# Test products of 12-bit operands and splitting operations behind the last product of a Fourier mixing and SwiGLU kernel

## The chip, the cores and the metric

One core of one Trainium2 chip. The metric is the device time of one execution in microseconds (us), the median of the runs shown.

## What is computed

The reference filters each sequence in the frequency domain and then applies a SwiGLU block to every token.

```python
batch, seq, dim = (8, 3008, 256)          # filter: 1505 frequencies x 256
X = np.fft.rfft(x, axis=1)
Y = X * (filt_r + 1j * filt_i)[None]
y = np.fft.irfft(Y, n=3008, axis=1).astype(np.float32)
x = y.reshape(24064, 256)                 # d_ff = 1536
g = x @ w_gate
silu = g * (1.0 / (1.0 + np.exp(-g)))
out = (silu * (x @ w_val) @ w_out).astype(np.float32)
```

## The kernel before, in words

The transform is factored: 3008 = 47 x 64, small table products in several stages, the spectrum multiplied with the filter in between, and the way back by the same kind of stages. The eight sequences are worked one after the other; while the SwiGLU block of one runs, the transform of the next is put in between in small pieces.

The SwiGLU block of a sequence is 12 steps: 4 chunks of tokens times 3 groups of hidden blocks. A `Group` object is one such step. Its products (`product`, line 1125) multiply combined weights in `wt_t` with the tokens `y` (P, Q) or with sums of them in `y_t` (A, B, E); 188 columns a product. ScalarE and VectorE turn the sums in PSUM into the hidden tile `h` (lines 1140 to 1172), VectorE and GpSimd combine `h` for the output (`S`, lines 312 and 315), and `project` (line 1223, 376 columns a product) multiplies with `wo_t` and adds into the output tile `o` on VectorE (line 312). Finished output tiles are transposed by VectorE (line 1194) and stored (line 1208).

The order of all this is written out by hand in the string `SCHEDULE`, one token an operation, and `pin` (`tc.keep_in_program_order`) holds every operation to that order on its engine. The work behind the last step stands in `LAST`: the rest of `S` and `W` (products), `o` (additions), `z1.o` and `z2.o` (transposes), `x0.o` to `X5.o` (stores, dealt in turn to the queues of SP, ScalarE and GpSimd, line 1208). The last operations of `LAST` are the end of the kernel. Nothing follows them.

Memory: `pool` opens a pool of tiles that lives to the end. `wo_t`, `wt_t`, `y_t` (128 x 18 x 188) and `lent` (128 x 7168) are whole-kernel tiles. The pools `hp` (four `h` buffers of 128 x 7 x 376), `np` (small tiles) and `op` (two output tiles) are opened late, when the start's own pool has closed. PSUM tiles come from `bank(name)`, eight banks in turn. `idle` (line 578) issues products that nobody reads; the kernel has 20 of them, all in its first 90 us. An unread ScalarE operation stands at line 1289.

All products have f32 operands. In the trace a product of f32 operands is two records, and so is its weight load.

Of the kernel before, what the change touches and what calls it, by code (L numbers as in the profile page):

```python
# [41 lines left out]
FP32 = mybir.dt.float32  # L42
U32 = mybir.dt.uint32
AF = mybir.ActivationFunctionType
ALU = mybir.AluOpType
# [155 lines left out]
def kernel(  # L201
# [10 lines left out]
    nc = tc.nc  # L212
# [10 lines left out]
    def pool(name, bufs, space=None):  # L223
        kw = {} if space is None else {"space": space}
        return ctx.enter_context(tc.tile_pool(name=name, bufs=bufs, **kw))
# [13 lines left out]
    y_t = cpool.tile([128, 3 * len(PAIRS), TQ], FP32)  # L239

    lent = cpool.tile([128, 14 * NV * C], FP32)
# [51 lines left out]
    pin = tc.keep_in_program_order  # L293
# [963 lines left out]
    with tc.tile_pool(name="start", bufs=1) as spool0:  # L1257
# [12 lines left out]
        n = 0  # L1270
        while n < NPR - 1:
            pair = ORDER[n][0] in "ABE" and ORDER[n + 1][0] in "ABE"
# [92 lines left out]
    def reload_sums(k, d):  # L1365
        pin(nc.sync.dma_start(out=sums_of(y_t, d), in_=sums_of(yt_dram[k], d)))

    hpool = pool("hp", 4)
    npool = pool("np", 1)
    opool = pool("op", 1)  # L1370

# [69 lines left out]
    for b in range(B):  # L1443
# [41 lines left out]
        for step in range(NCHUNK * NG + (b == B - 1)):  # L1485
# [16 lines left out]
            for place, token in enumerate(SCHEDULE):  # L1502
# [3 lines left out]
                op = token.rstrip("'")  # L1506
# [13 lines left out]
                elif op[0] == "t":  # L1520
                    n = int(op[1])
                    ps = pieces_before if old else pieces
# [21 lines left out]
                if b == 1 and step < 4 and op in FILTER_AT:  # L1544
                    n = FILTER_AT.index(op)
# [11 lines left out]
    for op in LAST:  # L1557
        if op[0] == "S":
            older.step(op, nc.gpsimd if op[1] == "2" else nc.vector)
        else:  # L1560
            older.project(op, True)
# [1 line left out]
_INS = ['x', 'filt_r', 'filt_i', 'moe_w_gate', 'moe_w_val', 'moe_w_out']  # L1563
_OUTS = [((B * S, C), 'float32')]
# [25 lines left out]
```

## Time and profile before

| | |
|---|---|
| two runs | 2789.07 and 2793.10 us |
| median | 2791.09 us |
| span of the profiled execution | 2788.6 us |
| the profiled execution's own time | not given beside its span |
| mean granted TensorE clock | 0.997 |
| end of TensorE's last product | 2779.6 us |
| end of VectorE's last operation | 2782.5 us |
| end of GpSimd's last store issue | 2786.0 us |

How to read the profile: times are microseconds from the start of the span, and ns where a mean is given. PE is TensorE's products, PEld its weight loads, DVE VectorE, ACT ScalarE, POOL GpSimd, and a name with q the engine's instruction queue. A line of groups has line, engine, operation, output and inputs with their shape, count, then busy us and mean ns of one, then the idle time ahead of them with what ended it. A line of the timeline has start, length and count; several equal instructions in a row are one line. A line of stretches has from and to, length, busy time and count of PE, PEld, DVE, ACT and POOL, the granted clock, the share of the DMA engines and GB/s.

### The profile page before, as it was taken

What the parts mean: (1) busy time and instruction counts of PE and PEld (TensorE: products, weight loads), DVE (VectorE), ACT (ScalarE), POOL (GpSimd) and SP (SyncE); (2) the same over time, 40 slices, a digit from 0 to 9 for tenths busy, and PEclk for the clock granted to TensorE, in tenths of its full rate; (3) what the DMA queues carried; (4) which work ended last, traced back from release to release, by engine and by line L of the source; (5) the groups of instructions that cost most, each with busy time, mean ns of one, the idle gap of its engine ahead of it and who ended that gap; (6) DMA issues with size and microseconds to landing.
All of it is one profiled execution on the core that took longest, in us unless ns stands there. A gap on an engine that the chain in (4) does not pass through costs nothing.

```text
span 2788.6 us, 51410 instructions
## 1 busy us (share of the span) xinstructions
PE 2748.3 (99%) x16952; PEld 2249.3 (81%) x16952; DVE 2081.7 (75%) x4703; ACT 1514.6 (54%) x4086; POOL 1647.4 (59%) x1801
## 2 busy tenths in 40 slices
PE   8999999999999999999999999999999999999998
PEld 6777887888878888788878888878887888888886
DVE  7888777777687777777778777777777777676666
ACT  5776454555555555555555555555554555555553
POOL 4786576566545665556654566555655566555554
PEclk9999999999999999999999999999999999999999
DMA  8688877878676776777767777668767677655543
GB/s 216 218 273 267 282 240 243 265 243 263 205 211 208 253 244 190 212 238 229 247 184 233 220 249 223 207 194 264 243 213 201 215 239 237 183 156 147 156 137 83
DMA packets 383488, 608.47 MB, mean 218 GB/s; under 512 B 197118, under 2 KB 266652, under 8 KB 383048
## 3 DMA queue, kind: packets, MB, share of 16 engines
q1 hardware_dynamic: 364410, 574.18, 65.9%
q10 hardware_dynamic: 16174, 25.50, 3.6%
q0 software_dynamic: 2640, 5.51, 0.7%
q8 instruction: 137, 2.24, 0.3%
q14 instruction: 127, 1.04, 0.1%
HBM read 484.45 MB, written 118.12 MB: 216 GB/s over the span
## 4 chain that ended last, share of the span: by engine, by line
PE 89%; DVE 3%; POOL 2%; ACT 1%; DMA 1%; issue 1%; SPq 0%; POOLq 0%; DVEq 0%; ACTq 0%
PE wa L1125 25%; PE wk L1125 17%; PE wA L1223 16%; PE we L1125 12%; PE wG L1223 8%; PE wF L1223 4%; PE wpd L1043 2%; PE wqc L807 1%; PE wqb L819 1%; PE wqa L727 1%; POOL h L315 0%; POOL out_dram L1208 0%; PE wpa L889 0%; DVE we L315 0%; DVE y L319 0%
## 5 line engine op out<-in xcount | busy, mean ns | idle before, releaser
L1125 PE MATMUL wa<-y_t,wt_t 128*128 128x188 f32 x4464 | 883.5, 324 | 10.5 <-DVE wa L1147 5.5
L1125 PEld LDWEIGHTS wa<-y_t,wt_t 128*128 128x128 f32 x4464 | 746.0, 190 | 102.9 <-issue 14.7
L1125 PEld LDWEIGHTS wk<-y,wt_t 128*128 128x128 f32 x2976 | 494.4, 190 | 125.2 <-issue 36.7
L1125 PE MATMUL wk<-y,wt_t 128*128 128x188 f32 x2976 | 575.6, 326 | 1.4 <-ACT f L1140 1.4
L315 POOL TENSOR_TENSOR h<-h 128x376 f32<-128x376 f32 x572 | 560.1, 1000 | 15.1 <-DVE h L312 14.9
L1223 PE MATMUL wA<-h,wo_t 128*128 128x376 f32 x1532 | 549.0, 481 | 3.4 <-POOL h L315 1.8
L1125 PE MATMUL we<-y_t,wt_t 128*128 128x188 f32 x2232 | 432.4, 323 | 2.4 <-DVE we L319 1.6
L315 POOL TENSOR_TENSOR D<-f,f 128x376 f32<-128x376 f32 x288 | 280.5, 985 | 252.0 <-ACT f L1140 245.4
L312 POOL TENSOR_TENSOR h<-h 128x376 f32<-128x376 f32 x190 | 183.2, 984 | 408.0 <-DVE h L1172 402.2
L315 DVE TENSOR_TENSOR we<-we,m 128x376 f32<-128x376 f32 x576 | 317.3, 552 | 91.6 <-PE we L1125 51.4
L1125 PEld LDWEIGHTS we<-y_t,wt_t 128*128 128x128 f32 x2232 | 369.1, 190 | 4.9 <-DVE we L319 2.8
L1223 PEld LDWEIGHTS wA<-h,wo_t 128*128 128x128 f32 x1532 | 278.0, 190 | 106.6 <-POOL h L315 5.4
L1160 ACT COPY m<-wa 128x376 f32<-128x376 f32 x576 | 275.4, 478 | 110.8 <-PE wa L1125 105.0
L1167 ACT ACTIVATE u<-we 128x188 f32<-128x188 f32 x576 | 188.9, 328 | 188.5 <-DVE we L315 179.1
L1223 PE MATMUL wG<-h,wo_t 128*128 128x376 f32 x768 | 273.9, 479 | 0.0
L319 DVE SCALAR_TENSOR_TENSOR y<-wk,c 128x376 f32<-128x376 f32 x480 | 246.7, 540 | 33.7 <-ACT c L1144 29.5
L1167 ACT ACTIVATE g<-wa 128x188 f32<-128x188 f32 x576 | 187.4, 326 | 143.8 <-PE wa L1125 141.6
L1144 ACT COPY c<-wk 128x376 f32<-128x376 f32 x288 | 136.9, 475 | 234.5 <-PE wk L1125 228.1
L1156 ACT COPY we<-y 128x376 f32<-128x376 f32 x480 | 218.9, 480 | 42.9 <-DVE y L1049 24.7
L1140 ACT ACTIVATE f<-wk 128x376 f32<-128x376 f32 x288 | 145.1, 504 | 168.6 <-PE wk L1125 108.3
L1172 DVE TENSOR_TENSOR h<-we,u 128x188 f32<-128x188 f32 x576 | 198.7, 345 | 35.1 <-ACT u L1167 21.9
L1172 DVE TENSOR_TENSOR h<-wa,g 128x188 f32<-128x188 f32 x576 | 196.1, 344 | 26.2 <-ACT g L1167 26.1
(194 smaller groups left out, 3532.0 us busy)
## 6 DMA issues: line engine op xcount, KB each, us to landing
wt_t<-w_all SPq DMA_DIRECT2D x174, 896.0 KB
wt_t<-w_all SPq DMA_DIRECT2D x174, 768.0 KB
lent<-filter SPq DMA_DIRECT2D x36, 1024.0 KB
quads<-lent SPq DMA_DIRECT2D x96, 256.0 KB
d<-lent ACTq DMA_DIRECT2D x84, 256.0 KB
t<-d SPq DMA_DIRECT2D x112, 192.0 KB
lent<-quads SPq DMA_DIRECT2D x144, 128.0 KB
lent<-raw SPq DMA_DIRECT2D x144, 128.0 KB
```

The source lines that it names most:

```text
L312: return eng.tensor_tensor(out=dst, in0=a, in1=b, op=ALU.add)
L315: return eng.tensor_tensor(out=dst, in0=a, in1=b, op=ALU.subtract)
L319: return nc.vector.scalar_tensor_tensor(out=dst, in0=a, scalar=-1.0, in1=b, op0=ALU.mult, op1=ALU.subtract)
L1043: pin(nc.tensor.matmul(out=outs_[h][32 * j:32 * j + 32, i], lhsT=back_t[0][r, ts(m, 32)], rhs=t[r, j], start=i == 0, stop=True, skip_group ...
L1125: pin(nc.tensor.matmul(out=ps[:, z], lhsT=self.wt[:, SLOT[p], z], rhs=rhs, start=start and z == 0, stop=True, skip_group_check=True))
L1140: pin(act.mul(self.small(f"f{i}", f"f{i}", 1), t[f"k{i}"], -1.0))
L1144: pin(act.copy(out=self.small(f"c{i}", f"c{i}", 1), in_=t[f"k{i}"]))
L1156: pin(act.copy(out=self.bank(f"e{at}"), in_=t[f"y{at}"]))
L1160: pin(act.copy(out=self.small(f"m{at}", "m", 4), in_=t[f"a{at}"]))
L1167: pin(act.activation(out=self.small(op, "g", 3, 1)[:, 0], in_=ps[:, 1], func=AF.Silu))
L1172: pin(v.tensor_tensor(out=dst, in0=ps[:, 0], in1=g, op=ALU.mult))
L1223: pin(nc.tensor.matmul(out=self.tiles[at], lhsT=wo_t[:, JB * q + i, WO[p], :], rhs=self.hs[i][:, HID[p]], start=start and i == 0, stop=Tru ...
```

## The change

The three late pools get an `ExitStack` of their own, which is closed behind `LAST`. In the room that they leave a pool `test` is opened with two tiles of the type F32R, a four-byte type whose values hold 12 significant bits. VectorE fills both (0 times `lent`, plus 0.75). TensorE runs 18 products each of 376, 188, 256 and 512 columns into one bank each, then 16 of 376 columns in turn into two banks. Then come three rounds of 14 operations on ScalarE, VectorE and GpSimd, which copy, multiply, apply Silu and split values into a 12-bit part and the rest; they write into `y_t` and the second test tile. Nothing of it is read for the output; output, products and stores ahead of it stay as they are.

```diff
-    hpool = pool("hp", 4)
-    npool = pool("np", 1)
-    opool = pool("op", 1)
+    late = ExitStack()
+
+    def late_pool(name, bufs):
+        return late.enter_context(tc.tile_pool(name=name, bufs=bufs))
+
+    hpool = late_pool("hp", 4)
+    npool = late_pool("np", 1)
+    opool = late_pool("op", 1)
...
             older.project(op, True)
+
+    late.close()
+    F32R = mybir.dt.float32r
+    tpool = pool("test", 1)
+    wr = tpool.tile([128, 768], F32R, name="test_w")
+    xr = tpool.tile([128, 1024], F32R, name="test_x")
+    pin(nc.vector.tensor_scalar(out=wr, in0=lent[:, 0:768], scalar1=0.0, scalar2=0.75, op0=ALU.mult, op1=ALU.add))
+    pin(nc.vector.tensor_scalar(out=xr, in0=lent[:, 0:1024], scalar1=0.0, scalar2=0.75, op0=ALU.mult, op1=ALU.add))
+    for n in (376, 188, 256, 512):
+        ps = bank(f"test_{n}")
+        for i in range(18):
+            pin(nc.tensor.matmul(out=ps[:, 0:n], lhsT=wr[:, ts(i % 6, 128)],
+                                 rhs=xr[:, 32 * i % 512:32 * i % 512 + n],
+                                 start=i == 0, stop=True, skip_group_check=True))
+    pair = [bank(f"test_pair_{i}") for i in range(2)]
+    for i in range(8):
+        for j in range(2):
+            pin(nc.tensor.matmul(out=pair[j][:, 0:376], lhsT=wr[:, ts(i % 6, 128)],
+                                 rhs=xr[:, 32 * i + 300 * j:32 * i + 300 * j + 376],
+                                 start=i == 0, stop=True, skip_group_check=True))
+    zt = y_t.rearrange("p s n -> p (s n)")
+    lam = 4096.0
+
+    def at(i, n=376):
+        return zt[:, 376 * i:376 * i + n]
+
+    stt = dict(scalar=-lam, op0=ALU.mult, op1=ALU.add)
+    hi, lo = xr[:, 0:376], xr[:, 376:752]
+    for r in range(3):
+        pin(nc.scalar.activation(out=at(0), in_=pair[0][:, 0:376], func=AF.Copy, scale=1.0 / lam))
+        pin(nc.vector.scalar_tensor_tensor(out=at(1), in0=pair[1][:, 0:376], scalar=1.0 + 1.0 / lam,
+                                           in1=at(0), op0=ALU.mult, op1=ALU.subtract))
+        pin(nc.scalar.activation(out=at(2), in_=at(1), func=AF.Silu))
+        pin(nc.vector.tensor_tensor(out=at(3), in0=at(1), in1=at(2), op=ALU.mult))
+        pin(nc.scalar.activation(out=hi, in_=at(3), func=AF.Copy, scale=1.0 - 2.0 ** -13))
+        pin(nc.gpsimd.tensor_tensor(out=lo, in0=at(3), in1=hi.bitcast(FP32), op=ALU.subtract))
+        pin(nc.vector.scalar_tensor_tensor(out=xr[:, 376:752], in0=lo.bitcast(FP32), in1=hi.bitcast(FP32), **stt))
+        pin(nc.gpsimd.tensor_tensor(out=at(5), in0=at(1), in1=at(2), op=ALU.mult))
+        pin(nc.vector.tensor_tensor(out=lo, in0=at(3), in1=hi.bitcast(FP32), op=ALU.subtract))
+        pin(nc.gpsimd.tensor_tensor(out=at(4, 752), in0=at(0, 752), in1=at(2, 752), op=ALU.subtract))
+        pin(nc.vector.tensor_tensor(out=at(6, 752), in0=at(0, 752), in1=at(2, 752), op=ALU.subtract))
+        pin(nc.scalar.activation(out=xr[:, 0:752], in_=at(4, 752), func=AF.Copy, scale=1.0 - 2.0 ** -13))
+        pin(nc.vector.tensor_scalar(out=hi, in0=at(3), scalar1=1.0 - 2.0 ** -13, scalar2=None, op0=ALU.mult))
+        pin(nc.gpsimd.tensor_scalar(out=hi, in0=at(3), scalar1=1.0 - 2.0 ** -13, scalar2=None, op0=ALU.mult))
```

## The prediction

> **What bounds the kernel now.** I read the page first, its busy shares and the chain that ended last.
>
> ```profile
> PE 2748.3 (99%) x16952; PEld 2249.3 (81%) x16952; DVE 2081.7 (75%) x4703; ACT 1514.6 (54%) x4086; POOL 1647.4 (59%) x1801
> ...
> PE 89%; DVE 3%; POOL 2%; ACT 1%; DMA 1%; issue 1%; SPq 0%; POOLq 0%; DVEq 0%; ACTq 0%
> ```
>
> TensorE is busy for 99% of the span and carries 89% of the chain. Cover from TensorE ends, though, where its last product ends, and everything that is added stands behind that point. So the timeline of the end comes second.
>
> ```profile
> 2770.85 1.43 PE L1223 MATMUL wF<-h,wo_t 128*128 128x376 f32 x4
> 2772.11 1.43 PE L1223 MATMUL wG<-h,wo_t 128*128 128x376 f32 x4
> ...
> 2778.18 1.43 PE L1223 MATMUL wG<-h,wo_t 128*128 128x376 f32 x4
> ...
> 2780.61 3.82 SPq L1208 DMA_DIRECT2D out_dram<-o  x8
> 2780.61 4.23 ACTq L1208 DMA_DIRECT2D out_dram<-o  x8
> ...
> 2781.50 1.04 DVE L1194 STREAM_TRANSPOSE o<-o 128x384 f32<-128x384 f32 x2
> 2783.00 3.05 POOL L1208 DMA_DIRECT2D out_dram<-o  x5 [0.28 <-issue]
> ```
>
> The reader is to see four ends: TensorE at 2779.6 us, VectorE at 2782.54, ScalarE's queue at 2784.84, GpSimd's last store issue at 2786.05. The span ends at 2788.6; the stores of this line take 1.9 to 2.5 us to land, which fills most of the last 2.55 us. All that can still cover added work is these 9 us.
>
> Third, the stretches, for the granted clock (the column after the five engines; the first three lines are the end, the last two the start of the kernel):
>
> ```profile
> 2782.00:2784.00 2.00, 0.00 (x0) 0.00 (x0) 0.54 (x2) 0.00 (x0) 1.72 (x4) 0.96 1.00 168
> 2784.00:2786.00 2.00, 0.00 (x0) 0.00 (x0) 0.00 (x0) 0.00 (x0) 2.00 (x4) 0.50 0.93 150
> 2786.00:2788.60 2.60, 0.00 (x0) 0.00 (x0) 0.00 (x0) 0.00 (x0) 0.06 (x1) 0.50 0.12 25
> ...
> 4.00:8.00 4.00, 4.00 (x22) 2.76 (x20) 0.00 (x0) 0.82 (x1) 0.00 (x0) 1.00 0.98 244
> ...
> 12.00:16.00 4.00, 4.00 (x22) 4.00 (x21) 2.02 (x7) 1.76 (x3) 1.10 (x3) 0.53 1.05 241
> ```
>
> By 2784 us the clock has fallen to 0.50. New products that begin there begin at half speed, as those at 12 us did.
>
> Fourth, the groups with shapes kept apart, for the durations:
>
> ```profile
> L1160 ACT COPY m<-wa 128x376 f32<-128x376 f32 x576 | 275.4, 478 | 110.8 <-PE wa L1125 105.0
> L1076 ACT ACTIVATE y_t<-y 128x376 f32<-128x376 f32 x64 | 29.4, 509 | 7.0 <-PE we L1125 7.0
> L319 DVE SCALAR_TENSOR_TENSOR y<-wk,c 128x376 f32<-128x376 f32 x480 | 246.7, 540 | 33.7 <-ACT c L1144 29.5 <-ACT we L1156 3.7 <-issue 0.2
> L315 POOL TENSOR_TENSOR h<-h 128x376 f32<-128x376 f32 x572 | 560.1, 1000 | 15.1 <-DVE h L312 14.9
> L312 POOL TENSOR_TENSOR y_t<-y 128x564 f32<-128x564 f32 x31 | 43.1, 1389 | 0.0
> ...
> L312 DVE TENSOR_TENSOR h<-h 128x376 f32<-128x376 f32 x2 | 1.0, 544 | 0.0
> ...
> L315 POOL TENSOR_TENSOR h<-h 128x376 f32<-128x376 f32 x2 | 2.4, 1216 | 14.9 <-DVE h L312 14.9
> ```
>
> **The change, part by part.** It removes nothing and moves no instruction. Giving the three late pools a stack of their own changes when they close and issues nothing; I cost it at zero. All else comes behind the last transpose on VectorE, the last product on TensorE, the last store issue on ScalarE's and GpSimd's queues. SP gets nothing.
>
> Step 1, two VectorE fills (768 and 1024 columns), which the products wait for. The TENSOR_SCALAR rows are 128x256: 283 ns the quickest, 611 in a large group. VectorE's additions grow by 1.01 ns a column (550 ns at 376, 740 at 564). At half of that slope the two take 0.54 + 0.67 = 1.2 us, at all of it 0.80 + 1.06 = 1.9, and from 611 ns 2.5. I take 1.5. They start at 2782.54, so the products start at 2784.1. The stores are still being issued meanwhile; nobody waits for these fills but TensorE.
>
> Step 2, 88 products: 18 each of 376, 188, 256 and 512 columns, 18 x 1332 = 23,976, and 16 of 376, 6,016; in all 29,992 columns. Before, each f32 product shows as two records: 20 idle products in the code stand as 40 records in the trace. Four records of 376 columns follow at 1.26 us, 0.84 ns a column and record. With two records each, as f32, the test takes 50.3 us; with one each at the same pace 25.2. From below, each product needs its weights: the shortest weight load of the trace (24x32, 103 ns) times 88 is 9.1 us. No row shows a product with such operands. The operands are narrower than f32's, so I put two records in a rival and take the middle of 9.1 and 25.2, 17.2 us. To that comes the clock: 32 equal records (L902) took 3.71 us at clock 1.00 and 6.38 at 0.53, 2.7 more; six records of 512 columns at the very start took 2.0 more than their warm pace; a half clock from 12 to 21.6 us would cost 4.8. I take 2.7. Products: 19.9 us, ending at 2804.0.
>
> Here a rule bears on the unknown. The Trainium skill, page "FP8 and Floating Point Precision", section "TensorE Precision Notes", says true FP32 takes four passes through the array and that there is a reduced form that truncates to a narrower float. The two records fit with four passes of two each. A single pass would be a quarter of 50.3, an estimate of 12.6 us, and the total 4.6 us lower. No run here shows that these operands take the reduced form.
>
> Step 3, three rounds of 14 operations. Nothing covers them: each round starts with ScalarE reading the pair that TensorE writes last, and the next round starts with ScalarE, behind its 752-column copy of the round before. The path through a round: ScalarE copy out of PSUM 0.48; VectorE 0.54; ScalarE Silu over 376, by the 376-column ACTIVATE, 0.51; VectorE product 0.54; ScalarE scaling 0.49; GpSimd difference 1.00. Together 3.56. Then GpSimd has its next two in its own order while VectorE runs three: a 376-column product and a 752-column difference. Alone the second takes 1.39 + 188 x 2.1 ns = 1.79; the row with VectorE beside it has 1.22 for 376, so 1.22 and 1.79 x 1.22 = 2.18. Then ScalarE's copy over 752: 509 ns and 376 x 0.78 (362 ns at 188) = 0.80. The sum is 7.76. Handoffs between engines in the chain of the end are 0.02 to 0.04 us, to GpSimd 0.15 to 0.28; seven in a round are 0.33. A round is 8.1 us, three 24.3. The last two, VectorE's scaling (0.45) and GpSimd's over the same tile (0.57, between its COPY rows of 390 ns for one column and 630 for 512), end the last round only, since otherwise they run beside ScalarE's and VectorE's next steps: 1.1 with handoffs. Step 3 is 25.4 us. Ends: GpSimd undisturbed (1.00 and 1.79) with short handoffs, 7.3 a round, 22.9 in all; VectorE and GpSimd taking strict turns, 3.56 + 0.54 + 1.00 + 0.54 + 1.79 + 0.94 + 0.80 + 0.33 = 9.5 a round, 29.6.
>
> On this the skill's page "SBUF — State Buffer", section "SBUF: two separate sides", has a rule that speaks against my sum: VectorE with two SBUF inputs and GpSimd take turns on one pair of ports, and the loser waits out the whole instruction. That would be the 29.6. The row is milder for GpSimd: 1.22 for 1.00 in the tail, while VectorE's two took 2.57 for 1.09. I stay with the row.
>
> Step 4, the end. The stores have long landed when the last operation ends, so of the 2.55 us only what is left over 1.9 to 2.5 of landing remains: 0.05 to 0.65. I take 0.5; the high end is 2.55.
>
> **The sum.** 2784.1 + 19.9 + 25.4 + 0.5 = 2829.9 against 2788.6: 41.3 us more span. The profiled execution shows its span, not its own total; the median of the two runs is 2.5 us over the span. I take that to stay: 2791.1 + 41.3 = 2832.4 us, 1.5% more.
>
> **Rivals.** First, two records for each test product, as before: 33.1 us more, 2865.5, 2.7% slower than before. For it: every product in this trace has two, whatever its shape. Against: the operands hold fewer bits. It decides once the products take over 31.7 us (17.2 and the 14.5 left to 2%), 0.36 us each on average; f32 would have 0.57. Chance 0.09.
>
> Second, a late start. The test tiles lie in memory of closed pools. They need 7 KB a partition and the first pool's first buffer has 10.5, read last by products long ended; that speaks for 2784.1. If instead the fills wait for the output tiles' stores, they start at 2786.05 + 2.3 = 2788.35, 5.75 later: 2838.1. Chance 0.14.
>
> Third, strict turns of VectorE and GpSimd: 4.2 more, 2836.6. Chance 0.10.
>
> Fourth, unread operations are left out and nothing changes: 2791. Against it: the unread idle products (40 records) and an unread ScalarE operation on a 128x1 tile at the start do stand in the trace. Chance 0.02.
>
> **How the numbers follow.** The forecast, 2832.4, has 0.63. Its own range is 2820.4 (2783.8 + 9.1 + 2.0 + 22.9 + 0.1, 29.3 more span) to 2840.4 (products at 25.2). Two high ends together, which reach 2846 and above, have 0.02. The range for 8 in 10 takes in the late start and the strict turns with part of their sums with 25.2: 2820 to 2847. 2%, 55.8 us or 2846.9, is about what a measurement of this kernel can tell from no change. Slower: 0.09 + 0.02, and 0.01 for prices that no row bounds, 0.12; faster: 0.01, since nothing is removed; same: 0.87.
>
> **What would show it.** One record for each test product, granted clock 0.5 at their start, about 20 us between the first and the last; ScalarE, VectorE and GpSimd idle for that time except the fills and the stores; then three equal rounds of about 8 us in which GpSimd has the most time, and an end within 1 us of GpSimd's last operation. Products up to 2779.6 us must stand as they do. Two records, a gap before the fills, or GpSimd operations well over 1.2 and 2.2 us would each prove a step wrong.

## The result, and the profile after

The changed kernel takes 2830.55 us (2829.24 and 2831.87) against 2791.09, 1.4% more by the medians; the ratio on record is 1.0149, 95% interval 1.0113 to 1.0184. That is clear of noise, though under the 2% that the prediction took as the line between slower and the same. The forecast was 2832.4. The profiled execution took 2829.24 us with a span of 2827.4; every run here stands 1.8 us over its span, not 2.5.

First the busy shares and the chain, from the page of the changed kernel:

```profile
PE 2764.3 (98%) x17040; PEld 2264.2 (80%) x17040; DVE 2098.9 (74%) x4723; ACT 1521.9 (54%) x4098; POOL 1662.4 (59%) x1813
...
PE 87%; DVE 3%; POOL 2%; ACT 2%; DMA 1%; issue 1%; SPq 0%; POOLq 0%; ACTq 0%; DVEq 0%
```

TensorE has 88 records more, 16952 and 17040: one for each of the 88 test products, so unread operations are not left out (the fourth rival). The chain that ended last, in order of time, then shows that nothing of the addition is hidden but the fills and the first products, which lie beside the stores:

```profile
2781.03 0.57 DVE test_w L1573
2781.60 0.60 DVE test_x L1574
...
2782.34 14.41 PE wtest L1578 x72
2796.75 2.58 PE wtest_pair L1584 x15
...
2799.36 0.49 ACT y_t L1596
...
2802.25 0.98 POOL test_x L1602
...
2803.25 1.32 DVE test_x L1603
...
2804.59 2.01 DVE test_x L1605
...
2806.71 0.83 ACT test_x L1608
2807.54 0.43 ACT y_t L1596
```

The last line is the second round's first operation. The chain counts it from the end of the operation ahead of it; in the timeline it starts at 2807.48, 8.12 us behind the first round's, and the third follows 8.20 later. The stretches give the clock, as in the prediction:

```profile
2782.00:2784.00 2.00, 1.66 (x5) 1.69 (x6) 0.20 (x1) 0.00 (x0) 2.00 (x4) 0.50 0.93 163
...
2786.00:2788.00 2.00, 2.00 (x8) 2.00 (x7) 0.00 (x0) 0.00 (x0) 0.00 (x0) 0.50 0.00 0
2788.00:2790.00 2.00, 2.00 (x18) 2.00 (x17) 0.00 (x0) 0.00 (x0) 0.00 (x0) 0.87 0.00 0
2790.00:2792.00 2.00, 2.00 (x20) 2.00 (x19) 0.00 (x0) 0.00 (x0) 0.00 (x0) 1.00 0.00 0
```

The granted clock falls to 0.50 at 2781.7 us, 3.6 us behind the last product of the old work, and steps to 1.00 at 2788.5 (hence the mean of 0.87 from 2788 to 2790). All 18 products of 376 columns, the last of which starts at 2787.8, ran at half clock, 0.313 us apart. At full clock the same width is 0.17 us apart (the 16 of the pair).

Last comes the timeline of VectorE and GpSimd in the second round, where the path parts from the one forecast:

```profile
2810.45 0.98 POOL L1602 TENSOR_TENSOR test_x<-y_t,test_x 128x376 fp32r<-128x376 f32 x1 [1.26 <-ACT test_x L1601]
2811.38 0.97 POOL L1604 TENSOR_TENSOR y_t<-y_t 128x376 f32<-128x376 f32 x1
2811.46 1.31 DVE L1603 SCALAR_TENSOR_TENSOR test_x<-test_x 128x376 fp32r<-128x376 f32 x1 [1.64 <-POOL test_x L1602]
2812.44 1.95 POOL L1606 TENSOR_TENSOR y_t<-y_t 128x752 f32<-128x752 f32 x1
2812.80 2.00 DVE L1605 TENSOR_TENSOR test_x<-y_t,test_x 128x376 fp32r<-128x376 f32 x1
2814.72 0.93 DVE L1607 TENSOR_TENSOR y_t<-y_t 128x752 f32<-128x752 f32 x1
```

GpSimd is hardly slowed (0.97 and 1.95 us), but VectorE's 376-column operations take 1.31 and 2.00 instead of 0.55. Each of them ends 0.4 us behind the GpSimd instruction that was running: 2811.38 + 0.97 = 2812.35 against 2812.77, and 2812.44 + 1.95 = 2814.39 against 2814.80. ScalarE's copy waits for VectorE (L1605), not for GpSimd.

Put against the forecast, each counted from the end of TensorE's last product (2779.6 us before, 2778.1 here):

| term | forecast us | measured us |
|---|---|---|
| to the first test product | 4.5 | 4.25 |
| 88 products | 19.9 | 17.0 |
| three rounds and the two last operations | 25.4 | 26.2 |
| end | 0.5 | 1.9 |
| sum | 50.3 | 49.3 |

The terms are 1.0 us under the forecast. Another 1.5 us is where the last product fell, and 0.7 the time over the span (1.8 for 2.5); together the profiled execution is 3.2 us under 2832.4. In the profiled executions of these runs it ended between 2776.8 and 2782.6 us, and once at 2789.6, with the same work ahead of it, so totals of single runs differ by that much.

### The profile page after: what moved, and what is told of

Its sections match the earlier page's. It is cut to its first block, busy times and chain, and to the rows that moved or that the text cites. A ratio compares the mean times of both kernels' runs of the same rounds, so it can differ in the third digit from the quotient of the medians.

```text
span 2827.4 us, 51641 instructions
## 1 busy us (share of the span) xinstructions
PE 2764.3 (98%) x17040; PEld 2264.2 (80%) x17040; DVE 2098.9 (74%) x4723; ACT 1521.9 (54%) x4098; POOL 1662.4 (59%) x1813
## 4 chain that ended last, share of the span: by engine, by line
PE 87%; DVE 3%; POOL 2%; ACT 2%; DMA 1%; issue 1%; SPq 0%; POOLq 0%; ACTq 0%; DVEq 0%
PE wa L1125 24%; PE wk L1125 16%; PE wA L1223 16%; PE we L1125 12%; PE wG L1223 8%; PE wF L1223 4%; PE wpd L1043 2%; PE wqc L807 1%; PE wqb L819 1%; PE wqa L727 1%; DMA lent<-later_tbl 1%; PE wtest L1578 1%; POOL h L315 0%; DVE we L315 0%; DVE y L319 0%
## 5 line engine op out<-in xcount | busy, mean ns | idle before, releaser
L1172 DVE TENSOR_TENSOR h<-wa,g 128x188 f32<-128x188 f32 x576 | 196.0, 344 | 26.2 <-ACT g L1167 26.1
```

What stands on the lines that cost most here:

```text
L1172: pin(v.tensor_tensor(out=dst, in0=ps[:, 0], in1=g, op=ALU.mult))
```

## The experiments

The theory after the result is that four terms stand in a row with nothing hidden but the fills, that the products are one record each and slowed at first by the clock, and that the rounds are set by VectorE waiting for GpSimd. The main rivals are two records (undecided by the trace of before), a start behind the stores, and a VectorE that is slow for another reason than GpSimd. Runs with an interval were compared with the kernel before on the same chip; of the others there is one execution each, read by its trace.

**Fills alone.** Products and rounds are left out.

```diff
     pin(nc.vector.tensor_scalar(out=xr, ...))
-    for n in (376, 188, 256, 512):
...
```

> Only the pools' own stack and the two fills are kept; test products and rounds are left out. Theory of the forecast (the fills lie under the stores): no change, 2791 us, VectorE's fills 0.64 and 0.67 us right behind the last transpose. Rival (the fills hold up GpSimd, which is issuing stores): up to 1.2 us more. Rival (closing the pools makes the fills wait for the stores): 5.7 us more.

Ratio 1.0004 (0.9994 to 1.0013). The timeline of its end:

```profile
2784.54 1.04 DVE L1194 STREAM_TRANSPOSE o<-o 128x384 f32<-128x384 f32 x2
2785.50 0.65 DVE L1573 TENSOR_SCALAR test_w<-lent 128x768 fp32r<-128x768 f32 x1
2786.04 3.27 POOL L1208 DMA_DIRECT2D out_dram<-o  x5 [0.28 <-issue]
2786.07 0.67 DVE L1574 TENSOR_SCALAR test_x<-lent 128x1024 fp32r<-128x1024 f32 x1
```

The fills start right behind the transpose, with the stores still being issued: no wait for the closed pools. GpSimd's five issues take 3.27 us, against 3.05 before; no time follows from it. The second rival of the prediction, the late start, falls.

**Products alone** (the loop `for r in range(3)` is left out) **and rounds alone** (two products, one for each bank of the pair, in place of 88).

> The rounds are left out, the 88 products stay. If the parts add up in a row: products 17.0 us from 4.25 us behind the last product, and a shorter end without GpSimd's last operation, so a span of about 2801 and 2803 us (0.4% more than before). Rival (the products hide under the stores to a larger part, and the rounds cost more than 26.2): below 2798.

Ratio 1.0047 (1.0032 to 1.0062), 2803.43 us: the parts stand in a row (4.25 us, then 15.8 of products), and the end without GpSimd is 1.0 us long.

> 86 of the 88 products are left out, one stays for each of the pair; the rounds stay. In a row: 16.2 us less than the whole change, 2814 us, rounds 8.2 us each. Rival (rounds depend on the clock or on the products before them): rounds longer or shorter than 8.2 by over 0.3 us.

2815.73 us, ratio 1.0092 (1.0065 to 1.0118); rounds of 8.14 and 8.21 us. They do not depend on the products. Products alone add 12.1 us and rounds alone 24.4, together less than the 39.5 of the whole change, mainly because each run alone uses the same 4.8 us beside the stores: before, the end came 9.0 us behind the last product, and the first test product starts 4.25 us behind it.

**Plain f32 operands.**

```diff
-    F32R = mybir.dt.float32r
+    F32R = FP32
```

> The whole change, but with test tiles of plain f32. If the operand type sets the number of records: two for each product and 50.3 us at full clock, 53 with half clock at the start, so 36 us more than the whole change, 2866. Rival (the product itself, its place or its constant values make it short): one record, 17 us, 2830.

2866.3 us, ratio 1.0277 (1.0255 to 1.0298). The groups with shapes kept apart, first of this run, then of the changed kernel (count, busy us, mean ns):

```profile
L1578 PE MATMUL wtest<-test_x,test_w 128*128 128x376 f32 x36 | 13.2, 532 | 4.2 <-DVE test_x L1574 4.2
...
L1578 PE MATMUL wtest<-test_x,test_w 128*128 128x188 f32 x36 | 5.9, 323 | 0.0
```

```profile
L1578 PE MATMUL wtest<-test_x,test_w 128*128 128x376 f32 x18 | 6.0, 523 | 4.3 <-DVE test_x L1574 4.3
...
L1578 PE MATMUL wtest<-test_x,test_w 128*128 128x188 f32 x18 | 2.3, 287 | 0.0
```

The type alone doubles the records; the products take 52.3 us from the first start to the last end against 53 expected (17.2 in the changed kernel, counted so). The profile still writes f32 for the narrow operands of TensorE; count and busy time tell the types apart. The prediction's first rival, two records for each product, had its price right (2865.5) and its condition wrong.

**The gap filled.** Five idle products hold TensorE busy until the fills are done.

```diff
     late.close()
+    idle(wt_t[:, 0:2].rearrange("p s z f -> p (s z f)"), [bank("idle") for _ in range(5)], 512)
```

> The whole change, with five idle f32 products of 512 columns (0.87 us each, 4.3 in all) put into TensorE's gap between the last product and the test products. Clock theory: granted clock 1.00 throughout, the first 18 products at 0.17 us instead of 0.313, products 14.4 us instead of 17.0, 2.6 less in all, 2828. Rival (the slow first 18 come from their weight loads or the fills): pace 0.313 stays, 2830.5.

```profile
2781.60 4.45 PE L578 MATMUL widle<-wt_t 128*128 128x512 f32 x10
2786.01 4.19 PE L1579 MATMUL wtest<-test_x,test_w 128*128 128x376 f32 x26
```

```profile
2785.00:2787.00 2.00, 2.00 (x9) 1.21 (x8) 0.87 (x2) 0.00 (x0) 1.83 (x3) 1.00 0.92 164
2787.00:2789.00 2.00, 2.00 (x13) 2.00 (x12) 0.00 (x0) 0.00 (x0) 1.44 (x3) 1.00 0.54 103
```

The granted clock stays at 1.00, the first 18 products follow at 0.17 us, and the products take 14.2 us instead of 17.0: the clock cost 2.8, as the 2.7 of the prediction had it. The total, 2828.81 us (1.0137, 1.0120 to 1.0154), can't be told from the changed kernel's by time alone; the trace decides. How long the half clock lasts varies from run to run: 8 of the 18 products in the run below with one operand on VectorE, 10 in the run with products alone, all 18 in the changed kernel. So this term is 1.3 to 2.8 us, and the changed kernel's is the longest. The clock fell 2.3 to 4.7 us behind the last product of the old work (the run without GpSimd's two and the run with the fills alone) and rose 2.9 to 6.2 us behind the first test product (the run with one operand and the changed kernel).

**GpSimd's two left out; VectorE's second operand from PSUM; VectorE with one operand.** Three edits of the same place:

```diff
-        pin(nc.gpsimd.tensor_tensor(out=at(5), ...))
-        pin(nc.gpsimd.tensor_tensor(out=at(4, 752), ...))
```

> GpSimd's two operations that run beside VectorE (the 376-column product and the 752-column difference) are left out of each round. If VectorE waits out GpSimd's whole instruction: its next two take 0.55 us each instead of 1.31 and 2.00, a round 5.9 instead of 8.2, 6.9 us less in all. Rival (VectorE is slow because it writes or reads 12-bit values): 1.31 and 2.00 stay, a round 8.2.

```diff
-... xr[:, 376:752], in0=lo.bitcast(FP32), in1=hi.bitcast(FP32), **stt))
+... xr[:, 376:752], in0=lo.bitcast(FP32), in1=pair[1][:, 0:376], **stt))
...
-... out=lo, in0=at(3), in1=hi.bitcast(FP32), op=ALU.subtract))
+... out=lo, in0=at(3), in1=pair[1][:, 0:376], op=ALU.subtract))
```

> GpSimd's operations stay; VectorE's two beside them take their second operand from PSUM instead of the test tile. If only VectorE instructions with two operands in the tile memory wait for GpSimd: 0.55 us each, and the path goes over GpSimd, 7.7 a round. Rival (any VectorE access beside GpSimd waits): 1.31 and 2.00 stay, 8.2 a round.

```diff
-        pin(nc.vector.scalar_tensor_tensor(out=xr[:, 376:752], in0=lo.bitcast(FP32), ...))
+        pin(nc.vector.tensor_scalar(out=lo, in0=lo.bitcast(FP32), scalar1=-lam, ...))
...
-        pin(nc.vector.tensor_tensor(out=lo, in0=at(3), in1=hi.bitcast(FP32), op=ALU.subtract))
+        pin(nc.vector.tensor_scalar(out=lo, in0=at(3), scalar1=-lam, ...))
```

> GpSimd's operations stay; VectorE's two beside them become scalings of one operand (0.36 us when alone). If one operand is enough to wait: about 1.1 and 1.8 us, 8.0 a round. Rival (only two operands wait): 0.36 each, path over GpSimd, 7.7 a round.

The timelines, without GpSimd, with PSUM, and with one operand:

```profile
2808.90 0.55 DVE L1603 SCALAR_TENSOR_TENSOR test_x<-test_x 128x376 fp32r<-128x376 f32 x1 [1.64 <-POOL test_x L1602]
2809.48 0.55 DVE L1604 TENSOR_TENSOR test_x<-y_t,test_x 128x376 fp32r<-128x376 f32 x1
```

```profile
2811.31 0.55 DVE L1603 SCALAR_TENSOR_TENSOR test_x<-test_x,wtest_pair 128x376 fp32r<-128x376 f32 x1 [1.64 <-POOL test_x L1602]
2811.89 0.55 DVE L1605 TENSOR_TENSOR test_x<-y_t,wtest_pair 128x376 fp32r<-128x376 f32 x1
2812.29 1.77 POOL L1606 TENSOR_TENSOR y_t<-y_t 128x752 f32<-128x752 f32 x1
2812.35 2.51 DVE L1607 TENSOR_TENSOR y_t<-y_t 128x752 f32<-128x752 f32 x1
2814.09 0.83 ACT L1608 ACTIVATE test_x<-y_t 128x752 fp32r<-128x752 f32 x1 [3.87 <-POOL y_t L1606]
```

```profile
2813.33 0.98 POOL L1604 TENSOR_TENSOR y_t<-y_t 128x376 f32<-128x376 f32 x1
2813.41 1.11 DVE L1603 TENSOR_SCALAR test_x<-test_x 128x376 fp32r<-128x376 f32 x1 [1.64 <-POOL test_x L1602]
2814.38 1.77 POOL L1606 TENSOR_TENSOR y_t<-y_t 128x752 f32<-128x752 f32 x1
2814.55 1.82 DVE L1605 TENSOR_SCALAR test_x<-y_t 128x376 fp32r<-128x376 f32 x1
```

Without GpSimd beside them the two take 0.55 us each and a round 5.9. With GpSimd there and one operand in PSUM they take 0.55 as well, and the path goes over GpSimd, 7.5 and 7.6 a round; now the 752-column operation, which still has two operands in the tile memory, waits (2.51 for 0.93) and ends 0.8 us behind GpSimd's. A scaling with one operand waits too, to 0.2 us behind GpSimd's instruction: 1.11 and 1.82 us instead of 0.36, 7.8 a round, near the 8.0 expected. So it is neither the 12-bit values nor VectorE's access as such: VectorE waits out the whole GpSimd instruction, with two operands in the tile memory, and also as a scaling from tile to tile. In all these pairs GpSimd had begun first, by 0.06 to 0.36 us. No run here has VectorE begin first ahead of a whole GpSimd instruction, and none tells why the scaling waits while an operation with one operand in PSUM does not.

**Widths.** The gap filled as above, and

```diff
-    for n in (376, 188, 256, 512):
+    for n in (64, 128, 188, 256):
```

> As the run with the gap filled, but with 64, 128, 188 and 256 columns in place of 376, 188, 256 and 512. If a weight load sets a floor under the pace of one-record products: 64, 128 and 188 all at 0.111 us, 256 at 0.118. Rival (a fixed cost and 0.43 ns a column, as 376 and 512 have it): 0.038, 0.065 and 0.091.

```profile
L1579 PE MATMUL wtest<-test_x,test_w 128*128 128x256 f32 x18 | 2.3, 283 | 0.0
L1579 PE MATMUL wtest<-test_x,test_w 128*128 128x128 f32 x18 | 2.2, 276 | 0.0
L1579 PE MATMUL wtest<-test_x,test_w 128*128 128x188 f32 x18 | 2.2, 275 | 0.0
L1579 PE MATMUL wtest<-test_x,test_w 128*128 128x64 f32 x18 | 2.2, 276 | 0.0
```

64, 128 and 188 columns cost the same, 0.111 us each from start to start (a record itself lasts longer, 0.28 us, since products overlap); 256 take 0.118. The floor is there, and the rival with a fixed cost and a price for each column falls. That it is the weight load fits the Trainium skill, page "TensorE: Matmul & The Clock Gate", section "LDWEIGHTS (loading the stationary operand)": its rule, columns over 1.2, gives an estimate of 107 ns for 128. No run here changed the loads themselves, and a fixed time to issue one load and one product would give the same flat row; so the floor is shown and its cause is only supported.

**Six rounds.** `range(3)` becomes `range(6)`.

> Six rounds instead of three. If the rounds stand in a row: 24.6 us more than the whole change, 2855. Rival (the rounds overlap or the first is dearer): under 22 us more.

2853.91 us, ratio 1.0228 (1.0209 to 1.0248); the first round takes 8.13 us and each of the later ones 8.21. They stand in a row.

**Other values.** The fills multiply by 1.0 and add 0.0.

> The test tiles hold 1.0 times what stands in the borrowed tile instead of 0.75 everywhere. If values do not matter to the pace: 17.0 us of products, 2830. Rival (varied values cost clock): granted clock below 1.00 after the first 6 us and longer products.

The products take 16.9 us, with full clock from 5.9 us behind the first. So it is not the constant values that make them short.

**The last operation.** `if r < 2:` ahead of GpSimd's scaling.

> GpSimd's scaling is left out of the last round, so VectorE's scaling is the last operation. If GpSimd's drain behind its own operation makes the end long: 0.85 us from the last operation to the end of the span instead of 1.86. Rival (a fixed end): 1.86 stays.

The last operation of this run (span 2826.8 us), then of the changed kernel (2827.4):

```profile
2825.55 0.36 DVE L1609 TENSOR_SCALAR test_x<-y_t 128x376 fp32r<-128x376 f32 x1
```

```profile
2824.42 1.15 POOL L1610 TENSOR_SCALAR test_x<-y_t 128x376 fp32r<-128x376 f32 x1 [1.83 <-DVE test_x L1609]
```

It is 0.90 us from VectorE's last operation to the end, against 1.9 behind GpSimd's in the changed kernel. So GpSimd as the last engine costs 1.0 us more behind its own operation.

## Why the prediction was right, point by point

- Nothing hides the addition, since it stands behind TensorE's last product: right. The fills alone add 0 us, products and rounds alone what a row of terms behind 4.25 us gives, and the terms of the changed kernel join end to start.
- Step 1, fills: right in place (4.25 against 4.5 us). They took 0.64 and 0.67 us, nearly the quick end.
- Step 2, one record for each product: right, and shown by the type alone. The term was mis-sized: 17.2 at full clock was the middle between two bounds, measured 14.2. The estimate of 12.6, worked out from the four passes that the Trainium skill, page "FP8 and Floating Point Precision", section "TensorE Precision Notes", gives true FP32, was nearer; in the runs 512 columns cost 0.86 us as f32 and 0.23 in the narrow type, 3.7 to 1. That 376 columns cost 0.17 us where the estimate has 0.158, and the floor at 188, make up most of the rest. The clock's 2.7 measured 2.8 here, but 1.3 to 2.8 over the runs, so the close match is in part luck.
- Step 3: the sum of a round (8.1 for 8.2) was right by a wrong path, and so by luck. "The row is milder for GpSimd", so the prediction let GpSimd slow down to 1.22 and 2.18 and put the path on it. That failed. GpSimd took 0.97 and 1.95, and the 3.40 us put on it were VectorE's 1.31 and 2.00, for which ScalarE waited. The end of the kernel before already showed such a wait:

```profile
2770.94 2.40 POOL L315 TENSOR_TENSOR h<-h 128x376 f32<-128x376 f32 x2 [14.87 <-DVE h L312]
2771.17 2.57 DVE L315 TENSOR_TENSOR h<-h 128x376 f32<-128x376 f32 x2
```

  VectorE's two took 2.57 us there for 1.09 and ended 0.4 us behind GpSimd's two. The Trainium skill's rule from "SBUF — State Buffer", section "SBUF: two separate sides", that the loser waits out the whole instruction, is what the runs show for VectorE. The price that the prediction gave it, 9.5 a round, was too high: it laid the instructions end to end, while VectorE's waits overlap GpSimd's work and only the 0.4 us behind the second is added; and it counted VectorE's 752-column difference (0.94), for which ScalarE's copy does not wait.
- The two last operations: GpSimd's scaling was put at 0.57 us, from its copies, and took 1.15.
- Step 4: "only what is left over" of the end, 0.5 us, failed. It was 1.9: 0.9 us follow the last operation when it is VectorE's, and 1.0 more when it is GpSimd's. What fills them, no run here shows.
- The misses, -2.9 on the products and +0.8 and +1.4 behind them, offset each other; so the total came closer than its terms did, which is luck.
- Two readings were slightly off, and nothing in the forecast hangs on them: the half clock at the start lasted to 22.5 us and not 21.6 (its mean from 20 to 24 us is 0.69), which would cost 5.1 us and not 4.8; and 2788.35 is 5.81 us behind 2782.54, not 5.75.

## What to carry to other kernels

Behind the last product every operation counts in full once the stores no longer cover it, so cost the tail as one chain. Count TensorE's first products there at half clock if it has stood still: here the clock fell 2.3 to 4.7 us behind the last product. Ahead of using 12-bit operands, count columns: with a new weight tile for each product, 376 columns cost 0.17 us instead of 0.63, 188 cost 0.11 instead of 0.32, and fewer still cost 0.11. Where VectorE and GpSimd must work side by side, look which of the two somebody waits for, and give VectorE an operand in PSUM (0.55 us here instead of 1.31 and 2.00).

## What was not expected of the hardware

GpSimd's scaling of one 376-column operand took longer (1.15 us) than its difference of two (0.97), in each round, also in the last, where VectorE had nothing left to do beside it. And the wait is not even: VectorE loses up to 1.6 us on an operation, while GpSimd's 752-column difference, which begins 0.33 us before VectorE's operation ends, loses 0.18 (1.95 against 1.77 with VectorE on PSUM).
